# Half-array matmuls gathered in two groups per slot, longer key and value rows, and a reordered entry in a fused attention and routed feed-forward kernel

## The chip, the cores and the metric

The kernel runs on one core of a Trainium2 chip. The metric is the device time of the whole kernel in microseconds (us). All data start and end in the chip's main memory.

## What is computed

```python
q_n = q / (norm(q) + 1e-06); k_n = k / (norm(k) + 1e-06)      # q, k, v: (8, 12, 448, 64), float32
scores = q_n @ k_n.T / tau                                    # tau 0.1
attn = softmax(scores); x = attn @ v                          # then x: (8, 448, 768)
for b in range(8):                                            # routed feed-forward
    s = x[b] @ w_gate
    top = the 128 tokens of largest s
    h = relu(x[b, top] @ w1)                                  # w1: 768 x 1024
    out[b] = x[b]; out[b, top] += sigmoid(s[top]) * (h @ w2)  # w2: 1024 x 768
```

## The kernel before

The 12 heads of a batch are taken in pairs, so there are 48 pairs, six to a batch. The main loop has 49 **slots**. Slot i does the scores and exponentials of pair i and the product with the values (PV) of pair i-1, prepares pairs further on, and carries a piece of the routed feed-forward (MoE) of an earlier batch. The order on every engine is the order in which the code is written; PE, DVE, ACT, POOL and the SP queue each work through their own list and wait on semaphores.

The 448 keys of a head are cut into three blocks of 128 and a tail of 64. Tails of the two heads sit in the lower and the upper 64 partitions of one block. A matmul on a tail, or on 64-row heads, uses half the array: it has a `tile_position`. In a slot PE runs

- `scores(i, c)`, c = 0 to 2 (L264): two half-array matmuls of 448 columns each, one per head; c = 3 (L269) is one full matmul on both tails. Each writes a `sc` tile; there are two of these buffers.
- `pv(i-1, u)` (L290, L293): for each head u and each of four row blocks, a half-array tail matmul, then three full ones, 65 columns each: 8 tails and 24 full ones in a slot.
- `transposes(i+1)` (L238, L233): four half-array (64 by 64) and six full ones into `qkT_ps`, copied by DVE (`qkT_copy`, L253) for the next slot's scores.
- `sum_pe` (L185): eight full matmuls that sum squares for the norms of a pair five slots on, into the free half of `sc(i, 3)`; DVE reduces them (`sum_dve`, L191).

ACT does `exps(i, c)` (L277, L280), `square` (L178) and, once per three pairs, two short norm instructions (L200, L201). DVE does `pv_evac` (L304, L305), which empties the PV result, and the routing arithmetic: `gate` (L327), `rank_count` (L366). POOL does `scale` (L217), `values` (L224) and `pick`. SP issues the loads: a group of three pairs in nine transfers, q, k and v in one large and two small ones each.

MoE pieces hang in a table, `at(slot, place, ...)`. Places "A" and "B" carry PE blocks: `rank_rep` (L354), `select`, `gather` (L425), `ffn1` (L439), `ffn2` (L452). In a slot "A" comes after `scores(i, 2)`, and "B" at the end, after `scores(i+1, 0)`, which is issued ahead. All MoE blocks share one PSUM bank (`m_ps`). Before the loop, an entry of five pairs loads and norms what the first slots need; after it the last batch's MoE runs alone.

## Time and profile before

| | |
|---|---|
| median of 2 runs | 522.43 us (522.36 to 522.5) |
| the profiled run | 518.5 us |
| its span, first to last instruction | 516.7 us |
| busy: PE, ACT, DVE, POOL | 449.1, 203.4, 181.0, 175.4 us |
| granted TensorE clock, mean | 0.779 |

Busy times are unions over the span; a busy PE is not PE at its peak, since matmuls overlap in it. The granted clock is a share of 2.4 GHz, and 0.50 means 1.2 GHz. The clock's first record in this trace comes after 100 us; stretches ahead of it are shown as 1.00.

### The profile page before, as it was taken

The page shows a single profiled execution, that of the slowest core. Times are in us where ns is not written, and L with a number is a line of the kernel's source. Part 1 is how long each engine was busy: PE and PEld are TensorE (multiplying, and loading weights), DVE is VectorE, ACT ScalarE, POOL GpSimd, SP SyncE. Part 2 cuts the span into 40 slices and gives each one's busy share as a digit, 9 for nine tenths or more (in the row PEclk, how much of TensorE's full clock was granted, in tenths as well). Part 3 has the DMA queues.
Part 4 walks back from the last instruction along what each step waited for, and adds up shares of the span by engine and source line. Part 5 has one row for each costly group of instructions (what it writes and reads, how often), then busy time and mean ns, then how long its engine had stood idle before and what let it go on. Part 6 is the DMA issues. An engine that isn't in the chain of part 4 may idle for free.

```text
span 516.7 us, 8595 instructions
## 1 busy us (share of the span) xinstructions
PE 449.1 (87%) x3537; PEld 273.1 (53%) x3537; DVE 181.0 (35%) x471; ACT 203.4 (39%) x291; POOL 175.4 (34%) x268
## 2 busy tenths in 40 slices
PE   2599998989999799979999799979998999899372
PEld 1355554545656457545665466545664565446250
DVE  1122223342262424442443425342444225334420
ACT  2463535344445335453453434543354433223000
POOL 2460415332425323360633323451534243310501
PEclk9999999985698657985787659875698567669556
DMA  6999759250666039250837048431502060020702
GB/s 164 283 283 251 166 124 242 60 148 1 157 164 178 15 107 213 58 138 1 214 108 190 1 127 195 117 75 41 122 1 31 1 159 3 0 32 1 190 1 30
DMA packets 64487, 56.78 MB, mean 110 GB/s; under 512 B 21568, under 2 KB 59968, under 8 KB 63424
## 3 DMA queue, kind: packets, MB, share of 16 engines
q1 hardware_dynamic: 59248, 44.21, 29.8%
q0 software_dynamic: 4768, 11.80, 14.9%
q8 instruction: 27, 0.44, 0.3%
q10 hardware_dynamic: 432, 0.23, 0.1%
q14 instruction: 12, 0.10, 0.1%
HBM read 39.71 MB, written 14.16 MB: 104 GB/s over the span
## 4 chain that ended last, share of the span: by engine, by line
PE 79%; DVE 12%; ACT 3%; SPq 2%; DMA 2%; issue 1%; POOLq 0%; POOL 0%; DVEq 0%; ACTq 0%
PE o_ps L293 18%; PE o_ps L290 10%; PE sc L264 9%; PE qkT_ps L233 9%; PE qkT_ps L238 6%; PE m_ps L425 6%; PE m_ps L452 6%; PE m_ps L439 5%; PE sc L185 4%; DVE junk L366 4%; DVE junk L327 3%; PE sc L269 3%; ACT expS L280 2%; PE m_ps L354 2%; DVE qkT L253 2%; DMA qk_raw<-in_k_dram 2%
## 5 line engine op out<-in xcount | busy, mean ns | idle before, releaser
L277 ACT ACTIVATE expS<-sc 128x896 bf16<-128x896 f32 x144 | 128.5, 915 | 173.2 <-PE sc L264 173.1
L293 PE MATMUL o_ps<-vo,expS 128*128 128x65 bf16 (+1 forms) x1152 | 118.8, 220 | 0.0
L217 POOL TENSOR_TENSOR qkn<-qk_raw,rs 128x512 bf16<-128x512 f32 x96 | 88.8, 954 | 54.3 <-ACT expS L277 27.8
L264 PE MATMUL sc<-qkT 64*128 64x448 bf16 x288 | 69.4, 472 | 27.3 <-ACT expS L280 22.7
L290 PE MATMUL o_ps<-vo,expS 64*128 64x65 bf16 (+1 forms) x384 | 84.9, 221 | 0.0
L293 PEld LDWEIGHTS <-expS 128*128 128x128 bf16 (+1 forms) x1152 | 66.3, 112 | 31.8 <-issue 14.4
L304 DVE RECIPROCAL rden<-o_ps 128x8 f32<-128x8 f32 x48 | 10.0, 208 | 159.3 <-PE o_ps L293 159.3
L233 PE MATMUL qkT_ps<-iden_b,qkn 128*128 128x128 bf16 x288 | 58.7, 267 | 0.5 <-POOL qkn L217 0.5
L280 ACT ACTIVATE expS<-sc 128x448 bf16<-128x448 f32 x48 | 26.1, 543 | 73.0 <-DVE ss L191 69.9
L290 PEld LDWEIGHTS <-expS 64*128 64x128 bf16 (+1 forms) x384 | 39.0, 102 | 24.0 <-issue 0.3
L185 PE MATMUL sc<-sq,iden_b 128*128 128x112 bf16 x384 | 39.9, 274 | 11.1 <-ACT sq L178 11.1
L178 ACT ACTIVATE sq<-qk_raw 128x896 bf16<-128x896 f32 x48 | 45.5, 952 | 9.1 <-DMA qk_raw<-in_k_dram 9.1
L238 PE MATMUL qkT_ps<-iden_b,qkn 64*64 64x64 bf16 x192 | 45.7, 238 | 2.5 <-POOL qkn L217 2.5
L185 PEld LDWEIGHTS <-iden_b 128*128 128x128 bf16 x384 | 34.9, 132 | 20.5 <-issue 19.1
L253 DVE COPY qkT<-qkT_ps 128x960 bf16<-128x960 bf16 x48 | 31.6, 658 | 37.7 <-PE qkT_ps L233 37.7
L264 PEld LDWEIGHTS <-qkT 64*128 64x128 bf16 x288 | 16.8, 98 | 52.0 <-issue 46.2
L458 POOL DMA_INDIRECT out_dram<-oe,idx x8 | 13.5, 1689 | 77.4 <-DVE oe L412 41.9
L452 PE MATMUL m_ps<-w_sb,hT 128*128 128x384 bf16 x128 | 35.1, 438 | 5.0 <-DVE junk L366 2.3
L318 POOL DMA_DIRECT2D xh<-x_b x8 | 5.0, 620 | 101.1 <-DVE x_b L305 101.1
L439 PE MATMUL m_ps<-xeT,w_sb 128*128 128x128 bf16 x384 | 32.8, 261 | 1.3 <-DVE hT L408 0.8
L305 DVE TENSOR_TENSOR x_b<-o_ps,rden 128x512 f32<-128x512 f32 x48 | 33.2, 691 | 1.7
L439 PEld LDWEIGHTS <-w_sb 128*128 128x128 bf16 x384 | 29.8, 121 | 6.2 <-issue 6.1
(70 smaller groups left out, 375.3 us busy)
## 6 DMA issues: line engine op xcount, KB each, us to landing
out_dram<-x_b SPq DMA_DIRECT2D x8, 1152.0 KB, 4.3
qk_raw<-in_q_dram SPq DMA_DIRECT2D x15, 576.0 KB, 6.4
qk_raw<-in_k_dram SPq DMA_DIRECT2D x15, 576.0 KB, 6.7
v_raw<-in_v_dram SPq DMA_DIRECT2D x15, 576.0 KB, 6.2
xh<-x_b POOLq DMA_DIRECT2D x8, 576.0 KB, 10.9
w_sb<-in_moe_w_dram POOLq DMA_DIRECT2D x2, 1536.0 KB, 12.8
out_dram<-x_b SPq DMA_DIRECT2D x8, 192.0 KB, 8.6
qk_raw<-in_q_dram SPq DMA_DIRECT2D x30, 48.0 KB, 5.8
```

The lines of the kernel that those rows point to most:

```text
L178: nc.scalar.activation(sq_tiles[p], raw[gi % NRAW][0][:, :, g].rearrange("p a b d -> p a (b d)") [:, :, :NB7 * Dh], AF.Square)
L185: nc.tensor.matmul(out=dst[:, :2 * NB7 * D8], lhsT=iden_b, rhs=sq[:, :, s * D8:(s + 1) * D8], start=(s == 0), stop=(s == Dh // D8 - 1))
L217: nc.gpsimd.tensor_mul(kn[:, :, :nb, o:o + Dh], qk[:, :, g, b0:b0 + nb], rs[:, g, :, b0:b0 + nb].rearrange("p a (b o) -> p a b o", o=1) .t ...
L233: nc.tensor.transpose(out=qkT_ps[:, o:o + P], in_=kn[:, a, c], identity=iden_b)
L238: nc.tensor.transpose(out=qkT_ps[r, o:o + T], in_=kn[r, a, NC, :Dh], identity=iden_b[r, r], tile_position=(u * T, u * T))
L253: nc.vector.tensor_copy(qkT_tiles[p], qkT_ps[:, :W])
L264: nc.tensor.matmul(out=sc[:, u, :S], lhsT=qkT[r, KO + c * P:KO + (c + 1) * P], rhs=qkT[r, :S], start=True, stop=True, tile_position=(u * D ...
L277: nc.scalar.activation(ex[:, 2 * c:2 * c + 2], sc[:, :, :S], AF.Exp, scale=inv_tau)
L290: nc.tensor.matmul(out=o, lhsT=ex[r, TAIL, cols], rhs=vo[r, NC], start=True, stop=False, tile_position=(u * T, 0))
L293: nc.tensor.matmul(out=o, lhsT=ex[:, 2 * c + u, cols], rhs=vo[:, u * NS + c], start=False, stop=(c == NC - 1))
L439: nc.tensor.matmul(out=ps[:, f * CAP:(f + 1) * CAP], lhsT=w1_sb[:, t, fc * P:(fc + 1) * P], rhs=xeT[:, t], start=(t == 0), stop=(t == KD - 1))
L452: nc.tensor.matmul(out=ps[:, :ND], lhsT=hT[:, t], rhs=w2_sb[:, t, n * ND:(n + 1) * ND], start=(t == 0), stop=(t == KF - 1))
```

## The change

**PE.** In a slot, `scores(i, 0)` and `scores(i, 1)` now stand together, then all eight PV tails (`pv_tails`, two heads in turn), then the 24 full PV matmuls. `scores(i, 2)` and the four 64 by 64 transposes stand together, then `scores(i, 3)`, the six full transposes, the sums, and "B". `scores(i+1, 0)` is no longer issued ahead of "B". The tail matmuls of a head open the whole accumulation bank once (`start` for j = 0 only).

**Other engines.** `exps(i, 3)` is issued before the sums and their reduction. Place "D" is split: "D1" ahead of `pv_evac`, "D2" behind it and ahead of `qkT_copy`; gates and rank counts are spread over both. "A" now comes right after `pv_evac`. `pick` moves one slot earlier. Some evacuations of the last two batches go to ACT.

**Loads.** Keys and values take another assignment of tokens to partitions: four tokens (1024 B) or three (768 B) in a row, in four transfers of 64 partitions per load. Queries are as before. The entry norms three pairs instead of five, starts slot 0 at once, and PE runs 80 matmuls on zeros (`warm`).

```diff
+    NORMS = [(0, 1), (1, 2), (3, 2)]
+    while sum(NORMS[-1]) < N:
+        NORMS.append((sum(NORMS[-1]), min(3, N - sum(NORMS[-1]))))
+    nplace = {g0 + g: (n, g) for n, (g0, gn) in enumerate(NORMS) for g in range(gn)}
...
-        eng.dma_start(
-            out=dst.rearrange("p g (u c) d -> p (g u) (c d)", c=4)[:, :, :NC * Dh],
-            in_=src[b, h0:h0 + nh, 0:SM, :].rearrange("h (m c) d -> m h (c d)", c=NC))
+        if which == 0:
+            eng.dma_start(
+                out=dst.rearrange("p g (u c) d -> p (g u) (c d)", c=4)[:, :, :NC * Dh],
+                in_=src[b, h0:h0 + nh, 0:SM, :].rearrange("h (m c) d -> m h (c d)", c=NC))
+            for u in range(2):
+                eng.dma_start(
+                    out=dst[u * T:u * T + T, :, NC],
+                    in_=src[b, h0:h0 + nh, SM:S, :].rearrange(
+                        "(g h) p d -> p g h d", h=2)[:, :, u])
+            return
+
+
         for u in range(2):
-            eng.dma_start(
-                out=dst[u * T:u * T + T, :, NC],
-                in_=src[b, h0:h0 + nh, SM:S, :].rearrange(
-                    "(g h) p d -> p g h d", h=2)[:, :, u])
-
-
...
+            for half in range(2):
+                n = NS if half == u else NC
+                b0 = 0 if u == 0 else NB7 - n
+                t0 = 0 if half == u else NS * T
+                eng.dma_start(
+                    out=dst[half * T:half * T + T, :, b0:b0 + n]
+                    .rearrange("p g c d -> p g (c d)"),
+                    in_=src[b, h0:h0 + nh, t0:t0 + n * T, :].rearrange(
+                        "(g h) (p c) d -> p g h (c d)", h=2, c=n)[:, :, u])
...
+    load(0, 0, nc.sync)
+    load(0, 1, nc.scalar)
+    nc.scalar.preload_act_table_set("natural_log_exp_and_others")
+    load(1, 0, nc.sync)
+    load(1, 1, nc.sync)
+    load(0, 2, nc.sync)
...
-        for b0, nb, o in ((0, NS, 0), (NS, NC, Dh)):
-            nc.gpsimd.tensor_mul(
+        for eng, b0, nb, o in zip(engines or (nc.gpsimd, nc.gpsimd),
+                                  (0, NS), (NS, NC), (0, Dh)):
+            eng.tensor_mul(
                 kn[:, :, :nb, o:o + Dh], qk[:, :, g, b0:b0 + nb],
...
-        tail(0, 0)
-        full(0, 0)
-        tail(0, 1)
-        full(0, 1)
-        tail(1, 0)
-        full(0, 2)
-        tail(1, 1)
-        for c in range(NC):
-            full(1, c)
+        if part == 0:
+            for a in range(2):
+                for u in range(2):
+                    tail(a, u)
+        else:
+            for a in range(2):
+                for c in range(NC):
+                    full(a, c)
...
-    def pv(i, u):
+
+
+    def pv_tails(i):
         ex = exp_tiles[i]
         vo = vo_bufs[i % NB]
-        r = slice(u * T, u * T + T)
         for j in range(NS):
             n = rows(j)
-            cols = slice(j * P, j * P + n)
-            o = o_ps[:n, u, j * E:(j + 1) * E]
-            nc.tensor.matmul(out=o, lhsT=ex[r, TAIL, cols], rhs=vo[r, NC],
-                             start=True, stop=False, tile_position=(u * T, 0))
-            for c in range(NC):
-                nc.tensor.matmul(out=o, lhsT=ex[:, 2 * c + u, cols],
-                                 rhs=vo[:, u * NS + c], start=False, stop=(c == NC - 1))
+            for u in range(2):
+                r = slice(u * T, u * T + T)
+                nc.tensor.matmul(out=o_ps[:n, u, j * E:(j + 1) * E],
+                                 lhsT=ex[r, TAIL, j * P:j * P + n], rhs=vo[r, NC],
+                                 start=(j == 0), stop=False, tile_position=(u * T, 0),
+                                 skip_group_check=True)
+
+    def pv(i):
+        ex = exp_tiles[i]
+        vo = vo_bufs[i % NB]
+        for u in range(2):
+            for j in range(NS):
+                n = rows(j)
+                for c in range(NC):
+                    nc.tensor.matmul(out=o_ps[:n, u, j * E:(j + 1) * E],
+                                     lhsT=ex[:, 2 * c + u, j * P:j * P + n],
+                                     rhs=vo[:, u * NS + c], start=False,
+                                     stop=(c == NC - 1), skip_group_check=True)
...
+    for b in range(B - 2):
         s = HP * (b + 1)
...
+        for j, (d, w) in enumerate(((1, "D1"), (1, "D2"), (2, "D1"), (2, "D2"))):
+            at(s + d, w, gate, b, j)
+        at(s + 3, "P", rank_prep, b)
+        at(s + 3, "B", rank_rep, b)
+        for j in range(NS):
+            at(s + 4, "D1" if j < 2 else "D2", rank_count, b, j)
+        at(s + 4, "P2", pick, b)
+        at(s + 5, "A", select, b)
+        at(s + 5, "C", select_b, b)
+        at(s + 5, "B", gather, b, 0)
+        at(s + 6, "A", gather, b, 1)
+        at(s + 6, "B", ffn1, b, 0)
+        late = b < B - 3
+        at(s + 7, "B" if late else "A", ffn1, b, 1)
+        at(s + 7 + late, "B", ffn2, b, 0)
+        at(s + 8 + late, "A", ffn2, b, 1)
...
+    at(s + 2, "B0", rank_rep, b)
...
+    at(s + 6, "A", ffn1, b, 1, "A")
+    at(s + 6, "A", ffn2, b, 0, "A")
+    at(s + 6, "A", ffn2, b, 1, "A")
...
+    SQ = {}
+    for p in range(3, N):
+        SQ.setdefault({3: 0, 4: 0, 5: 1, 6: 1}.get(p, p - 5), []).append(p)
+    SW = 2 * NB7 * D8
...
+    warm(30)
...
+            warm(50)
+            scale(0, (nc.gpsimd, nc.vector))
...
+            scores(i, 0)
             scores(i, 1)
+        if prev:
+            pv_tails(i - 1)
+            pv(i - 1)
+        if live:
             exps(i, 0)
             exps(i, 1)
+            for p in SQ.get(i, []):
+                square(p)
+        run(i, "D1")
         if prev:
-            pv(i - 1, 0)
-            pv(i - 1, 1)
             pv_evac(i - 1)
-        if nxt:
-            transposes(i + 1)
-            qkT_copy(i + 1)
-        run(i, "D")
+        run(i, "A")
+        run(i, "D2")
+        run(i, "P2")
         if i + 2 < N:
             scale(i + 2)
             values(i + 2)
         if live:
             scores(i, 2)
-            if i + LA < N:
-                square(i + LA)
-            exps(i, 2)
-        run(i, "A")
+        if nxt:
+            transposes(i + 1, 0)
         if live:
             scores(i, 3)
-            if i + LA < N:
-                sc = sc_tiles[i, 3]
-                sum_pe(i + LA, sc[:, 1])
-                sum_dve(i + LA, sc[:, 1])
+        if nxt:
+            transposes(i + 1, 1)
+            qkT_copy(i + 1)
+        if live:
+            exps(i, 2)
+            sc = sc_tiles[i, 3]
             exps(i, 3)
-            gi, g = place.get(i + LA, (0, -1))
-            if g == GROUPS[gi][1] - 1:
-                norm_a(gi)
-                norm_b(gi)
+            for m, p in enumerate(SQ.get(i, [])):
+                dst = sc[:, 1, m * SW:(m + 1) * SW]
+                sum_pe(p, dst)
+                sum_dve(p, dst)
+                n, g = nplace[p]
+                if g == NORMS[n][1] - 1:
+                    norm_a(n)
+                    norm_b(n)
         run(i, "C")
-        run(i, "E")
-        if nxt:
-            scores(i + 1, 0)
+        run(i, "B0")
         run(i, "B")
```

On PE, at the end of the first slot with `rank_rep` (L354, now L384), before. L264 is `scores`, L290 a PV tail, L293 a full PV matmul.

```order
L264 LDWEIGHTS qkT [waits DVE_49]
L264 MATMUL sc<-qkT 128x448 [waits Activation_49]
...
L354 MATMUL m_ps<-diag,ones_f 128x448 [waits Pool_49]
L357 MATMUL m_ps<-gate_145,iden_f 128x4
...
L264 MATMUL sc<-qkT 128x448 [waits Activation_49]
...
L290 MATMUL o_ps<-vo_138,expS 128x65
L293 LDWEIGHTS expS
L293 MATMUL o_ps<-vo_138,expS 128x65
...
L290 MATMUL o_ps<-vo_138,expS 128x65
```

One score pair is issued ahead of the MoE block, one behind it, and tails alternate with runs of three. And now (L203 sums, L282 `scores`, L309 a tail, L321 a full PV matmul):

```order
L203 MATMUL sc<-sq,iden_b 128x112
L384 MATMUL m_ps<-diag,ones_f 128x448 [waits Pool_49]
L387 MATMUL m_ps<-gate_151,iden_f 128x4
L282 LDWEIGHTS qkT [waits DVE_49]
L282 MATMUL sc<-qkT 128x448 [waits PE_49]
...
L282 MATMUL sc<-qkT 128x448 [waits DVE_49]
...
L309 MATMUL o_ps<-vo_144,expS 128x65
...
L321 MATMUL o_ps<-vo_144,expS 128x65
```

All four score matmuls stand behind the MoE block, the tails follow them, and the full matmuls come in one run.

On PE, from the end of PV to the third and fourth scores in a plain slot, before (L238 and L233 are half and full transposes):

```order
L238 LDWEIGHTS qkn_136 [waits Pool_49]
L238 MATMUL qkT_ps<-iden_b,qkn_136 64x64
L233 LDWEIGHTS qkn_136 [waits Pool_49]
L233 MATMUL qkT_ps<-iden_b,qkn_136 128x128
...
L238 MATMUL qkT_ps<-iden_b,qkn_136 64x64
...
L233 MATMUL qkT_ps<-iden_b,qkn_136 128x128
...
L264 MATMUL sc<-qkT 128x448 [waits Activation_49]
...
L269 MATMUL sc<-qkT 128x448 [waits Activation_49]
```

Half and full transposes alternate there, ahead of the scores. The same stretch now, up to the sums (L257 and L252 are the transposes):

```order
L282 MATMUL sc<-qkT 128x448 [waits Activation_49]
...
L257 LDWEIGHTS qkn_142 [waits Pool_49]
L257 MATMUL qkT_ps<-iden_b,qkn_142 64x64
...
L287 MATMUL sc<-qkT 128x448 [waits Activation_49]
L252 LDWEIGHTS qkn_142 [waits Pool_49]
L252 MATMUL qkT_ps<-iden_b,qkn_142 128x128
...
L203 MATMUL sc<-sq,iden_b 128x112 [waits Activation_49]
```

The half transposes moved behind the third score pair, and the full ones follow the full score matmul without a half-array one between.

On DVE, the second slot with gates of a batch, before (L304, L305 `pv_evac`; L253 `qkT_copy`; L327 `gate`; L191 `sum_dve`):

```order
L304 RECIPROCAL rden<-o_ps 128x8 [waits PE_49]
L305 TENSOR_TENSOR x_b<-o_ps,rden 128x4x128 [waits DVE_49]
L253 COPY qkT<-qkT_ps 128x960 [waits PE_49]
L327 ISA junk,gate_145<-x_b,wg_b 128x768
L327 ISA gate_145 128x1
L327 ISA junk,gate_145<-x_b,wg_b 64x768 [waits DVE_49]
L327 ISA gate_145 64x1
L191 TENSOR_REDUCE ss<-sc 128x14 [waits PE_49]
```

Both gates stand behind the copy there. The same slot now (L334, L335; L271; L357; L209, in the same roles):

```order
L357 ISA junk,gate_151<-x_b,wg_b 128x768 [waits DVE_49]
L357 ISA gate_151 128x1
L334 RECIPROCAL rden<-o_ps 128x8 [waits PE_49]
L335 TENSOR_TENSOR x_b<-o_ps,rden 128x4x128 [waits DVE_49]
L357 ISA junk,gate_151<-x_b,wg_b 64x768
L357 ISA gate_151 64x1
L271 COPY qkT<-qkT_ps 128x960 [waits PE_49]
L209 TENSOR_REDUCE ss<-sc 128x14 [waits PE_49,Activation_49]
```

One gate moved ahead of `pv_evac` and one ahead of `qkT_copy`, and the reduction of the sums now waits on ACT.

## Rows read from the trace of the kernel before

**Rows 1.** The page, part 4: the chain that ended last, by engine.

```profile
PE 79%; DVE 12%; ACT 3%; SPq 2%; DMA 2%; issue 1%; POOLq 0%; POOL 0%; DVEq 0%; ACTq 0%
```

**Rows 2.** Stretches, a slot each: length; PE PEld DVE ACT POOL busy; clock; DMA; GB/s.

```profile
40.29:48.88 8.59, 8.13 (x58) 4.57 (x58) 1.83 (x4) 3.91 (x5) 0.56 (x1) 1.00 1.12 229
...
150.03:157.70 7.67, 7.05 (x66) 4.42 (x65) 3.57 (x8) 4.39 (x6) 3.44 (x8) 1.00 0.05 13
...
167.22:176.92 9.70, 6.77 (x58) 4.11 (x57) 4.41 (x12) 3.92 (x5) 5.24 (x9) 0.78 0.19 35
176.92:188.09 11.17, 11.17 (x82) 6.45 (x82) 3.11 (x10) 4.15 (x6) 0.00 (x0) 0.50 0.00 0
```

**Rows 3.** Timeline of PE, an early slot: start, length, instruction, [idle before].

```profile
48.77 0.26 PE L238 MATMUL qkT_ps<-iden_b,qkn 64*64 64x64 bf16 x1
...
50.62 0.56 PE L264 MATMUL sc<-qkT 64*128 64x448 bf16 x2
...
51.46 0.95 PE L185 MATMUL sc<-sq,iden_b 128*128 128x112 bf16 x8
...
53.68 0.26 PE L290 MATMUL o_ps<-vo,expS 64*128 64x65 bf16 x1
53.87 0.35 PE L293 MATMUL o_ps<-vo,expS 128*128 128x65 bf16 x3
...
57.37 0.26 PE L238 MATMUL qkT_ps<-iden_b,qkn 64*64 64x64 bf16 x1
```

**Rows 4.** Timeline of PE, a later slot.

```profile
149.93 0.21 PE L238 MATMUL qkT_ps<-iden_b,qkn 64*64 64x64 bf16 x1
...
151.26 0.36 PE L264 MATMUL sc<-qkT 64*128 64x448 bf16 x2
...
151.76 0.56 PE L185 MATMUL sc<-sq,iden_b 128*128 128x112 bf16 x8
...
152.93 1.47 PE L452 MATMUL m_ps<-w_sb,hT 128*128 128x384 bf16 x8
...
154.90 0.19 PE L290 MATMUL o_ps<-vo,expS 64*128 64x65 bf16 x1
155.02 0.27 PE L293 MATMUL o_ps<-vo,expS 128*128 128x65 bf16 x3
...
157.60 0.21 PE L238 MATMUL qkT_ps<-iden_b,qkn 64*64 64x64 bf16 x1
```

**Rows 5.** The chain in order of time, MoE blocks on PE: start, length.

```profile
163.21 0.95 PE m_ps L354 x2
...
181.52 2.61 PE m_ps L425 x16
...
193.42 2.68 PE m_ps L439 x24
...
470.25 1.46 PE m_ps L439 x24
...
482.68 1.86 PE m_ps L354 x2
```

**Rows 6.** Waits: us in total, times, longest.

```profile
ACT expS L280 <- DVE ss L191: 69.9, 43, 3.2
```

**Rows 7.** Groups by line and shape, DVE: busy, mean ns | idle before.

```profile
L305 DVE TENSOR_TENSOR x_b<-o_ps,rden 128x512 f32<-128x512 f32 x48 | 33.2, 691 | 1.7
...
L253 DVE COPY qkT<-qkT_ps 128x960 bf16<-128x960 bf16 x48 | 31.6, 658 | 37.7 <-PE qkT_ps L233 37.7
...
L327 DVE CUSTOM_DVE_ANT_0 junk<-x_b,wg_b 128x768 bf16<-128x768 f32 x21 | 20.0, 952 | 0.3
```

**Rows 8.** The chain again, the square that ends the entry.

```profile
19.39 0.96 ACT sq L178
```

**Rows 9.** Line L304, the first evacuation instruction of each pair: first and last start.

```profile
L304 DVE RECIPROCAL rden<-o_ps x48: 206/208/209, 31.7 to 478.8; 128x8 f32<-128x8 f32 x48
```

**Rows 10.** Loads: KB each, median us from issue to landing.

```profile
qk_raw<-in_k_dram SPq DMA_DIRECT2D x15, 576.0 KB, 6.7
```

More of the change, by code (lines that the diff above doesn't have):

```diff
@@ L184, in sum_pe @@
         for s in range(Dh // D8):
-            nc.tensor.matmul(out=dst[:, :2 * NB7 * D8], lhsT=iden_b,
+            nc.tensor.matmul(out=dst, lhsT=iden_b,
                              rhs=sq[:, :, s * D8:(s + 1) * D8],
@@ L226, with transposes @@
     qkT_tiles = {}
-    def transposes(p):
+    def transposes(p, part):
         kn = kn_bufs[p % NB]
@@ L414, in evac, with gather @@
             nc.scalar.activation(dst, src, func, scale=scale)
-    def gather(b, part):
+    def gather(b, part, eng="D"):
         sel, xh = st[b]["sel"], xh_tiles[b]
@@ new lines @@
+        late = b < B - 3
+        at(s + 7, "B" if late else "A", ffn1, b, 1)
+        at(s + 7 + late, "B", ffn2, b, 0)
+        at(s + 8 + late, "A", ffn2, b, 1)
+    b, bb = B - 2, B - 1
+    s = HP * bb
+    for j, (d, w) in enumerate(((0, "D2"), (1, "D1"), (1, "D1"), (1, "D2"))):
+        at(s + d, w, gate, b, j)
+    at(s + 2, "P", rank_prep, b)
+    at(s + 2, "B0", rank_rep, b)
+    for j in range(NS):
+        at(s + 3, "D1" if j < 2 else "D2", rank_count, b, j)
+    at(s + 3, "P2", pick, b)
```

153 lines of the change are left out of this document (60 added, 93 removed).

## The prediction

> **What bounds the kernel now.** I first read the page's chain of waits: 79% of the span is PE [rows 1], so PE's own work and PE's order set the time. Then I cut the span into slots, from one first evacuation instruction (L304) to the next. There are 48, the first at 31.7 us and the last at 478.8 [rows 9], so the span of 516.7 is 31.7 of entry, 47 intervals of 9.51 on average, and 37.9 behind the last one. The intervals differ by two things, the MoE blocks in them and TensorE's clock [rows 2]: a plain slot takes 8.59 with PE busy for 8.13, a slot with one feed-forward block 7.67, a slot with two gathers 11.17.
>
> The clock has to be read from lengths early on. The stretch at 40.29 is shown with a granted clock of 1.00 [rows 2], but the eight sums take 0.95 in the slot after it, and 0.56 a hundred us later, where 1.00 is shown too [rows 2 to 4]. A feed-forward block of 24 matmuls takes 2.68 at 193.42, soon after a slot at 0.50, against 1.46 late in the kernel [rows 2, 5], much the same ratio. So the early part ran at the lower level, 1.2 GHz, and the early slots are slow for that. Later the kernel changes between the levels: the slot at 176.92 has PE busy for its whole length and a clock of 0.50, the one at 150.03 has 1.00 [rows 2].
>
> Last come PE's rows inside a slot. PV takes 2.70 at the high level (154.90 to 157.60) and 3.69 at the low one (53.68 to 57.37), though it is only 32 matmuls of 65 columns [rows 3, 4]. Three full ones in a row need 0.27 (0.35 low) from first start to last end, while one alone takes about 0.19 to 0.24: they start about 0.04 (0.06) apart. The step from a tail to a full matmul takes 0.12 (0.19). PE pays for changes between half and full array, sixteen of them in PV and eight in the transposes.
>
> **The change part by part.**
>
> *PV.* After: 24 full ones and 8 tails at 0.04 and one change of 0.12, 0.96 + 0.32 + 0.12 + 0.05 for the narrow blocks = 1.45; it saves 1.25 at the high level. At the low one 24 x 0.06 + 8 x 0.06 + 0.19 = 2.1, saving 1.6. No row shows tails of the two heads next to each other. The two score matmuls of a pair end in 0.36 together, so half matmuls of different halves do overlap [rows 4]; the bounds are 0.16 for the eight (in pairs) and 8 x 0.12. I take 0.32.
>
> The Trainium skill speaks against this term (TensorE: Matmul & The Clock Gate, "Back-to-back issue gap": in a stream of weight load and matmul pairs, about 81 ns each for 128 columns). By that figure the 24 would take 1.9 us, an estimate, and the total would come out a few us later. This trace does not agree: 24 feed-forward matmuls of 128 columns in 1.46 us are 61 ns each [rows 5].
>
> *Transposes.* 1.33 now at the high level, 1.85 at the low one (149.93 to 151.26, 48.77 to 50.62) [rows 3, 4]. After: six full ones at 0.061 (0.112), four half ones at 0.04 (0.05), one change: 0.65 (1.07). It saves 0.68 (0.78).
>
> *PE in a plain slot.* High: 7.05 busy at 150.03, less the feed-forward block of 1.47 [rows 2, 4], is 5.6; less 1.93 is 3.65. Low: 8.13 less 2.4 is 5.75.
>
> *The new chain.* Now ACT matters. The order makes `exps(i, 3)` come before the sums, and both use the tile `sc(i, 3)`. Before, with the opposite order, `exps(i, 3)` waited for the reduction of the sums, 69.9 us in 43 slots [rows 6]; that wait goes. What is late next is its mirror image: the sums wait for `exps(i, 3)`, and the "B" block, the next score pairs and their exponentials are queued behind the sums on PE. One round is: first score pair 0.36 (0.56), ACT's five instructions 3.91 in a plain slot [rows 2], sums 0.56 (0.95), four hand-overs of about 0.05. That is 5.0 (5.6). PE alone needs 3.65 (5.75), so a plain slot takes 5.0 at the high level, bound by ACT and the hand-overs, and 5.7 at the low one, bound by PE. Before, `scores(i+1, 0)` was ahead of "B" and ACT worked under "B"; now "B" adds its length in full. B blocks of a batch, high: `rank_rep` 0.95, a gather of 16 (estimated from the 24 in 1.46) 1.0, three feed-forward blocks at 1.46, together 6.3 or 1.06 a slot; low: 1.86 + 2.61 + 3 x 2.68 = 12.5, 2.1 a slot [rows 5]. "A" blocks lie beside ACT's exponentials; I charge 0.2 (0.4). Two norm instructions every third slot add about 0.15, and DVE and POOL in the slots of rank counts and `pick` 0.15: DVE's row from PV's end to the next scores is evacuation 0.69 + 0.21, a gate 0.95, the copy 0.66 [rows 7], 2.5, and fits in 5.0 behind a PV that ends at about 2.1. Sum: **6.55 us a slot with MoE at the high level, 8.45 at the low one.** Bounds: no extra waits at all 6.0; nothing below, since ACT's 3.91, the sums and "B" are rows.
>
> *Which level.* Runs of full matmuls become the rule, which speaks for the high level: the blocks that ran at 1.46 to 1.47 did so behind such runs. Against it: in a high slot PE ends its transposes after about 3.0 us and waits until 4.5 for the sums, and in the slot at 167.22, where PE was busy for 6.77 of 9.70, the clock was 0.78 and then 0.50 [rows 2]. I take a mixture of two thirds high: 7.2 a slot with MoE, 5.4 a plain one.
>
> *Entry.* Before, the squares of pair 3 start at 19.39, when their keys arrive [rows 8]. The bytes ahead of them are the same after; slot 0 now runs before, and these squares come inside it. From 19.39: two squares 1.8, two exponentials 1.4, two sums 1.9, scores and PV 3.1: the first evacuation at 27.7. Slot 1 then waits for group 3, which is asked for no earlier, and the second comes at 35.4, where before it was at 31.7 + 8.6 = 40.3. Longer rows carry the same bytes in eleven transfers a group instead of nine; 576 KB land in 6.7 us [rows 10] against three slots of lead, so I count nothing, hidden by that lead. The 80 warm matmuls cost nothing either while PE waits for the first keys; without that cover the 50 would cost 50 x 0.11 = 5.6. Splitting `scale(0)` over POOL and DVE and moving one exponential of the gates are below 1 us.
>
> *End.* 37.9 before. In the last slot three feed-forward blocks now share the single bank with the last `rank_rep`, and their evacuations go through ACT: some 4 us more. Evacuations in turn on ACT and DVE give back about 1. I take 41.
>
> *Sum.* 35.4 to the second evacuation, 7 plain intervals at 5.4 = 37.8, 39 with MoE at 7.2 = 280.8, end 41: a span of 395. The span of before stands to the median of the runs as 516.7 to 522.43, a factor of 1.011: **about 399 us**.
>
> **The rivals.**
>
> *The clock stays high* (0.25): 35.4 + 7 x 5.0 + 39 x 6.55 + 40 = 365.9, or 370 us. For it: blocks and runs are denser than anything in the early slots. Against: the pause of about 1.5 in each slot. With no extra waits, 6.0 a slot, it is 349.
>
> *The clock stays low* (0.15): 35.4 + 7 x 5.7 + 39 x 8.45 + 43 = 447.9, or 453 us. For it: the early slots had PE busy for 8.13 of 8.59 and never left that level.
>
> *The gathering does not do what it says* (0.08): each full PV matmul waits for its weight load. The wait is then bounded by a feed-forward matmul of 0.112 at the low level, so 24 x 0.07 = 1.7 more, of which ACT's slack of about 1.1 in the middle of the slot hides most; 0.6 a slot comes through, 28 us: 427. Three starts in 0.27 speak against it [rows 4].
>
> *Slower than before* (0.03): the loads. Each transfer on SP's queue waits for the one eight before it, so a group of eleven takes 11/8 of a landing time. It decides from a landing of 15.7 us, when that equals three slots of 7.2; for more than 533 us the slots must be 10.6, a landing of 23. Rows show 6.7 [rows 10], so 64-partition transfers would have to be over three times slower.
>
> **How the numbers follow.** The forecast has 0.47, its own range 378 to 425. The rest (0.02) is spread out. From 358 to 450 lie the forecast, most of the high case, the ungathered case and half of the low one, about 0.8. A change of 2% is about what a measurement of this kernel can tell from none. All cases but the last are faster by more, so 0.95; slower 0.03; the rest 0.02.
>
> **What would show it.** In the profile after: PV in a slot at 1.4 to 1.5 us (high), the transposes at about 0.65, the wait of the fourth exponential for the reduction gone, and in its place a wait of the sums' matmuls for `exps(i, 3)`; plain slots between 5.0 and 5.7; the mean clock between 0.6 and 0.9. Wrong would be: sums that start without waiting, a clock at one level throughout, or slots bounded by DVE, POOL or the loads.

## The result and the profile after

The changed kernel takes **370.57 us**, median of 2 runs (369.96 to 371.18), against 522.43: a ratio of 0.709 with a 95% interval of 0.704 to 0.714. The forecast was 399 and its range 358 to 450. The time is that of the rival in which the clock stays high (370). The medians here and below leave out runs that lie more than 1.5% above the fastest of the same kernel; ranges have every run.

| stage of the span | forecast | profile after |
|---|---|---|
| first, second evacuation of PV, at | 27.7, 35.4 | 30.8, 38.5 |
| 7 plain intervals | 37.8 | 40.2 |
| 39 intervals with MoE | 280.8 (7.2 each) | 249.6 (6.40 each) |
| behind the last evacuation | 41 | 41.1 |
| span | 395 | 369.4 |

The first evacuation instruction of each pair again (line L334 now, L304 in [rows 9]): 48, from 30.8 to 328.3. Below they are counted from 0: evacuation 0 ends the entry, and evacuation 8 the plain intervals.

```profile
L334 DVE RECIPROCAL rden<-o_ps x48: 196/207/209, 30.8 to 328.3; 128x8 f32<-128x8 f32 x48
```

Part 4 of the page, the chain that ended last; it answers to [rows 1]. PE had 79%, and no engine now has half.

```profile
PE 34%; ACT 19%; DVE 14%; DMA 13%; issue 12%; SPq 3%; POOL 2%; POOLq 1%; DVEq 0%; ACTq 0%
```

Stretches of the changed kernel, with the columns of [rows 2]: first the stages (entry, first interval, 7 plain ones, 38 with MoE, end; the 39th with MoE, 6.35, lies between the last two), then five neighbouring slots.

```profile
0.00:30.82 30.82, 17.92 (x186) 14.88 (x186) 6.08 (x28) 12.32 (x19) 10.64 (x24) 0.82 0.78 195
30.82:38.47 7.65, 6.78 (x67) 4.64 (x65) 2.11 (x6) 4.77 (x7) 5.29 (x9) 0.50 1.07 259
38.47:78.71 40.24, 31.07 (x401) 20.90 (x399) 18.54 (x42) 27.40 (x41) 19.65 (x29) 0.81 1.07 246
78.71:321.96 243.25, 200.65 (x2764) 141.27 (x2763) 168.81 (x363) 148.99 (x217) 134.26 (x193) 0.96 0.64 148
328.31:369.40 41.09, 18.25 (x140) 12.20 (x139) 7.66 (x27) 3.62 (x7) 8.98 (x14) 0.73 0.31 70
...
161.68:166.74 5.06, 3.80 (x60) 2.61 (x58) 3.03 (x9) 3.89 (x7) 4.33 (x7) 1.00 1.04 235
166.74:172.93 6.19, 5.55 (x83) 4.04 (x82) 4.60 (x13) 4.29 (x10) 2.49 (x4) 1.00 0.64 165
172.93:182.51 9.58, 7.78 (x122) 5.99 (x122) 7.37 (x9) 6.09 (x9) 8.35 (x11) 1.00 0.84 214
182.51:186.96 4.45, 2.89 (x54) 2.25 (x51) 3.98 (x11) 1.56 (x2) 0.48 (x1) 1.00 1.06 279
186.96:195.16 8.20, 7.69 (x66) 4.48 (x65) 3.94 (x10) 4.63 (x9) 1.96 (x6) 0.58 0.42 106
```

A slot without a block takes 5.06, and PE is busy in 3.80 of it. The granted clock over the 38 MoE slots is 0.96: if 1.00 is the high level and 0.50 the low one, 8% of the stretch was low. The five rows also show something that the prediction had not foreseen: once in a batch an interval of 9.58 stands beside one of 4.45. Here a low stretch comes right behind that pair. It does so behind two of the five pairs (0.78 and 0.58); behind the other three the clock is 1.00, and 7.78 us of the low time lie in one slot near the end (314.18 to 321.96).

PE's timeline of one slot; it answers to [rows 4].

```profile
177.22 0.55 PE L282 MATMUL sc<-qkT 64*128 64x448 bf16 x4
177.61 0.40 PE L309 MATMUL o_ps<-vo,expS 64*128 64x65 bf16 x8
177.94 1.27 PE L321 MATMUL o_ps<-vo,expS 128*128 128x65 bf16 x24
179.14 0.36 PE L282 MATMUL sc<-qkT 64*128 64x448 bf16 x2
179.44 0.25 PE L257 MATMUL qkT_ps<-iden_b,qkn 64*64 64x64 bf16 x4
179.62 0.36 PE L287 MATMUL sc<-qkT 128*128 128x448 bf16 x1
179.82 0.50 PE L252 MATMUL qkT_ps<-iden_b,qkn 128*128 128x128 bf16 x6
181.47 0.55 PE L203 MATMUL sc<-sq,iden_b 128*128 128x112 bf16 x8 [1.16 <-ACT expS L298]
```

PV, from 177.61 to 179.14, is 1.53 (2.70 before); the transposes are 0.25 + 0.50 (1.33 before). The sums now wait for the fourth exponential. The list of waits has that as a whole; the wait of [rows 6] is not in it.

```profile
ACT expS L295 <- PE sc L282: 92.0, 55, 4.6
...
PE sc L203 <- ACT expS L298: 41.4, 41, 5.9
```

The pair of 9.58 and 4.45 is told by two engines' timelines between 175 and 183. VectorE:

```profile
177.32 0.69 DVE L438 TENSOR_SCALAR hT<-m_ps 128x512 bf16<-128x512 f32 x1 [1.00 <-PE m_ps L469]
177.93 4.64 DVE L357 CUSTOM_DVE_ANT_0 junk<-x_b,wg_b 128x768 bf16<-128x768 f32 x1
182.51 0.20 DVE L334 RECIPROCAL rden<-o_ps 128x8 f32<-128x8 f32 x1
```

GpSimd:

```profile
174.16 0.63 POOL L348 DMA_DIRECT2D xh<-x_b  x1 [4.93 <-DVE x_b L335]
...
175.33 1.86 POOL L236 TENSOR_TENSOR qkn<-qk_raw,rs 128x512 bf16<-128x512 f32 x2
177.11 0.57 POOL L243 CAST vo<-v_raw 128x448 bf16<-128x448 f32 x1
177.63 1.84 POOL L236 TENSOR_TENSOR qkn<-qk_raw,rs 128x512 bf16<-128x512 f32 x2
179.42 0.55 POOL L243 CAST vo<-v_raw 128x448 bf16<-128x448 f32 x1
179.93 1.82 POOL L236 TENSOR_TENSOR qkn<-qk_raw,rs 128x512 bf16<-128x512 f32 x2
181.71 1.27 POOL L243 CAST vo<-v_raw 128x448 bf16<-128x448 f32 x1
```

GpSimd first idles for 4.93 ahead of a store of x that waits for the evacuation, then has three pairs' scale and values in a row. The first gate of the batch (0.95 in [rows 7]) takes 4.64, nearly as long as that row lasts, and the evacuation of a PV that ended at 179.14 stands behind it until 182.51. It happens in five batches (4641 to 4675 ns). In the first batch the profile has the gate wait 4.49 for its weights `wg_b` beside the same row, and the interval is 9.52.

### The profile page after: what moved, and what is told of

The parts are those of the page before. It is cut to its first block, busy times and chain, and to the rows that moved or that the text cites. A ratio compares the mean times of both kernels' runs of the same rounds, so it can differ in the third digit from the quotient of the medians.

```text
span 369.4 us, 8858 instructions
## 1 busy us (share of the span) xinstructions
PE 281.0 (76%) x3617; PEld 198.5 (54%) x3617; DVE 206.6 (56%) x476; ACT 198.5 (54%) x291; POOL 178.8 (48%) x267
## 4 chain that ended last, share of the span: by engine, by line
PE 34%; ACT 19%; DVE 14%; DMA 13%; issue 12%; SPq 3%; POOL 2%; POOLq 1%; DVEq 0%; ACTq 0%
ACT expS L295 12%; DMA qk_raw<-in_q_dram 7%; PE o_ps L321 7%; PE m_ps L482 6%; PE m_ps L455 5%; PE sc L282 5%; PE sc L203 4%; DVE junk L357 4%; ACT sq L196 3%; DMA wg_b<-in_moe_w_gate_dram 3%; DVE junk L396 3%; SPq L114 3%; ACT expS L298 3%; PE m_ps L469 3%; DVE qkT L271 2%
## 5 line engine op out<-in xcount | busy, mean ns | idle before, releaser
L236 POOL TENSOR_TENSOR qkn<-qk_raw,rs 128x384 bf16<-128x384 f32 (+1 forms) x95 | 91.8, 1032 | 26.0 <-DVE rs L226 12.8
L321 PE MATMUL o_ps<-vo,expS 128*128 128x65 bf16 (+1 forms) x1152 | 64.5, 202 | 0.0
L203 PE MATMUL sc<-sq,iden_b 128*128 128x112 bf16 x384 | 29.5, 226 | 45.8 <-ACT expS L298 41.4
L282 PE MATMUL sc<-qkT 64*128 64x448 bf16 x288 | 50.5, 383 | 15.2 <-DVE qkT L271 13.2
L321 PEld LDWEIGHTS <-expS 128*128 128x128 bf16 (+1 forms) x1152 | 51.2, 104 | 10.0
L203 PEld LDWEIGHTS <-iden_b 128*128 128x128 bf16 x384 | 25.7, 105 | 51.8 <-issue 51.1
L357 DVE CUSTOM_DVE_ANT_0 junk<-x_b,wg_b 128x768 bf16<-128x768 f32 (+3 forms) x32 | 48.3, 1510 | 4.6 <-DMA wg_b<-in_moe_w_gate_dram 4.5
L271 DVE COPY qkT<-qkT_ps 128x960 bf16<-128x960 bf16 x48 | 31.3, 652 | 14.8 <-PE qkT_ps L252 14.8
L334 DVE RECIPROCAL rden<-o_ps 128x8 f32<-128x8 f32 x48 | 9.9, 206 | 45.7 <-PE o_ps L321 45.6
L243 POOL CAST vo<-v_raw 128x448 bf16<-128x448 f32 x48 | 35.1, 731 | 0.5 <-DMA v_raw<-in_v_dram 0.5
L335 DVE TENSOR_TENSOR x_b<-o_ps,rden 128x512 f32<-128x512 f32 x48 | 33.2, 691 | 1.7
L209 DVE TENSOR_REDUCE ss<-sc 128x14 f32<-128x112 f32 x48 | 13.0, 272 | 31.8 <-PE sc L203 31.3
L366 POOL TENSOR_TENSOR diag<-iden_f,gate 128x512 f32<-128x512 f32 x8 | 8.9, 1117 | 41.4 <-DVE gate L357 41.4
L282 PEld LDWEIGHTS <-qkT 64*128 64x128 bf16 x288 | 12.6, 95 | 29.7 <-DVE qkT L271 16.6
L405 POOL TENSOR_SCALAR sel<-iota_r,rank 128x128 bf16<-128x128 bf16 (+1 forms) x32 | 22.7, 854 | 10.8 <-DVE junk L396 10.1
```

The lines of the kernel that those rows point to most:

```text
L203: nc.tensor.matmul(out=dst, lhsT=iden_b, rhs=sq[:, :, s * D8:(s + 1) * D8], start=(s == 0), stop=(s == Dh // D8 - 1))
L236: eng.tensor_mul(kn[:, :, :nb, o:o + Dh], qk[:, :, g, b0:b0 + nb], rs[:, m, :, b0:b0 + nb].rearrange("p a (b o) -> p a b o", o=1) .to_broa ...
L243: nc.gpsimd.tensor_copy(vo_bufs[p % NB][:, :, :Dh], raw[gi % NRAW][1][:, g, :NB7])
L271: nc.vector.tensor_copy(qkT_tiles[p], qkT_ps[:, :W])
L282: nc.tensor.matmul(out=sc[:, u, :S], lhsT=qkT[r, KO + c * P:KO + (c + 1) * P], rhs=qkT[r, :S], start=True, stop=True, tile_position=(u * D ...
L321: nc.tensor.matmul(out=o_ps[:n, u, j * E:(j + 1) * E], lhsT=ex[:, 2 * c + u, j * P:j * P + n], rhs=vo[:, u * NS + c], start=False, stop=(c ...
```

## The experiments

**The theories.** A: the gathering is the gain, through shorter PE work and through the high level. B: the gain is the new order (exponentials ahead of the sums, blocks ahead of the next scores, entry), and the gathering lies in ScalarE's shadow. For the 9.58: GpSimd's row keeps the gate out, or the gate only shows another wait. "38 slots" below is the stretch between evacuations 8 and 46, with its mean granted clock, in the run that has the trace (436.7 us for PV alone, 380.7 for the transposes alone). The kernel before took 505.3 to 523.9 beside these runs, with medians of 517.5 to 519.8, so a few us between two rows of the table are not resolved. The edits are shown shortened.

| kernel | us, median (lowest to highest) | 38 slots, us | clock there |
|---|---|---|---|
| before | 522.4 | 368.1 | 0.74 |
| all but the gathering | 464.5 (461.6 to 464.5) | 317.0 | 0.77 |
| PV alone as it was | 430.3 (430.1 to 442.9) | 294.5 | 0.82 |
| gathering alone | 394.0 (393.9 to 398.5) | 282.8 | 0.77 |
| sums first | 385.0 (383.6 to 386.0) | 254.6 | 0.81 |
| transposes alone as they were | 378.3 (376.0 to 383.1) | 245.6 | 0.95 |
| changed | 370.6 (370.0 to 371.2) | 243.3 | 0.96 |
| old entry | 370.0 (369.2 to 371.5) | 242.1 | 0.97 |
| short rows | 367.2 (365.0 to 368.9) | 242.1 | 0.97 |
| gate behind the evacuation | 364.6 (362.9 to 365.9) | 237.9 | 0.98 |
| gate behind the copy | 360.7 (357.3 to 361.4) | 237.3 | 0.95 |
| entry, stores and gate | 355.3 (355.0 to 360.9) | 229.0 | 0.98 |
| stores of x behind values | 352.8 (351.9 to 360.9) | 228.2 | 1.00 |
| entry, stores and gate, scores ahead | 381.1 (379.8 to 383.4) | 256.9 | 0.89 |

**PV as it was, the rest changed.**

```diff
-            pv_tails(i - 1)
-            pv(i - 1)
+            # per (u, j): the half matmul (start=True), then its three full ones
```

> The changed kernel, with only PV as it was: each (u, j) opens its own sum with its half-array matmul and adds its three full ones, where pv stands now; everything else as changed. Theory A (the gathering is the gain, and the short slots keep the clock high): PV takes 2.7 us in place of about 1.5 in each slot; 39 MoE slots of 6.40 become 7.65 and the plain ones rise by about 0.6, so 424 at the same clock, and 440 to 480 if the granted clock falls from 0.89 to 0.8 or less. Rival B (the gain is the new order of exps, sums and scores, and the entry; the gathered PV only lies in the shadow of ScalarE): PV still reads 2.7, but the time is 375 to 390 and the clock stays near 0.89.

430.3 us, ratio to before 0.834 (0.819 to 0.849). PE's timeline has the old alternation at the old price: PV from 243.70 to 246.40, 2.70.

```profile
243.70 0.19 PE L314 MATMUL o_ps<-vo,expS 64*128 64x65 bf16 x1
243.82 0.27 PE L317 MATMUL o_ps<-vo,expS 128*128 128x65 bf16 x3
...
246.40 0.33 PE L411 MATMUL m_ps<-tokc,sel 128*128 128x2 bf16 x4
```

The stretch of that slot, and the whole 38 slots:

```profile
240.43:246.51 6.08, 4.82 (x60) 3.23 (x58) 2.94 (x9) 3.91 (x5) 4.33 (x6) 1.00 1.01 270
...
91.56:386.06 294.50, 274.85 (x2764) 185.03 (x2763) 157.21 (x364) 150.85 (x216) 131.45 (x190) 0.82 0.50 115
```

Theory A holds and B falls, though the time lies between A's two cases (424, and 440 to 480). A plain slot at the high level is 6.08 against 5.06; 1.02 over 47 intervals would be 48 of the 60 us lost. The remaining 12 stand beside a lower clock: 0.80 over the whole of the two runs that make the median, against 0.89.

**The transposes as they were, the rest changed.**

```diff
-        if part == 0: the four half transposes
-        else: the six full ones
+        if part == 0: return
+        tail, full, tail, full, tail, full, tail, full, full, full
```

> The changed kernel, with only the transposes in their old alternation of half and full, all behind scores(i, 3). Theory A: 0.68 us more on TensorE in each slot (1.33 against 0.65), in 39 MoE slots that are bounded by TensorE: 371 + 27 = 397, half that (384) if the transposes' wait for the scale hides part. Rival B: they lie before the wait for exps, so they are hidden: 370 to 374. The granted clock stays at 0.85 or more in both.

378.3 us, below A's bounds and above B's. The 38 slots hardly move (245.6 against 243.3), as B expected. In the traced run the loss is ahead of them: evacuation 8 comes at 87.6 in place of 78.7, and the early slots stay at the low level with PE busy throughout, 6.75 each for four of them:

```profile
38.86:65.84 26.98, 26.96 (x230) 16.59 (x228) 8.57 (x20) 16.16 (x24) 8.07 (x11) 0.50 1.05 222
```

That is the rival in which the clock stays low, for 50 us. Why it stays low there is not shown.

**Both as they were.** The two edits above together.

> The changed kernel with PV and the transposes both in their old alternation; the order of the slot, the entry and the loads stay as changed. Theory A: 1.25 + 0.68 us more per slot over 39 MoE slots and less over the plain ones: 450 at the same clock, and up to 500 if the clock falls to about 0.7 as the longer slots idle; most of the 152 us gained is lost again. Rival B: 380 to 395, so that four fifths of the gain stay.

464.5 us, ratio 0.898 (0.887 to 0.910): all the rest of the change is worth 55 us without the gathering. On top of PV, the transposes cost 34 and not 8: PE is busy in 312.5 of the 317.0 us of the 38 slots, so nothing hides them.

**The gathering alone, in the kernel before.**

```diff
-            pv(i - 1, 0)
-            pv(i - 1, 1)
+            pv_tails(i - 1)
+            pv(i - 1)
```

(and `transposes` with its four half ones ahead of its six full ones)

> The kernel before with the gathering alone: PV's eight half-array matmuls opened together and the transposes in two groups, at the places where pv and transposes stood; the order of the slot, the entry, the loads and the MoE's places stay as before. Theory A (the gathering is worth the same anywhere): 464 - 371 = 94 us, the difference between the changed kernel with and without it, so 428. Interaction (it pays in full only if ScalarE no longer waits for the sums behind scores(i, 3)): the slots stay bounded by that wait, and TensorE idles and falls to its low level: 470 to 500. A third: the gathering alone brings the high level and nearly all of the gain, 385 or less.

394.0 us, ratio 0.768 (0.765 to 0.771): 125 us, more than either of the first two cases expected and less than the third. The parts do not add up: 125 and 55 alone, 152 together. The wait of [rows 6] is still there, with 36 of its 43 times:

```profile
ACT expS L277 <- DVE ss L191: 66.5, 36, 4.5
```

So that wait did not hold the kernel before; PE did. Plain slots take 4.35 here, less than the changed kernel's 4.75 to 5.06. From here to the changed kernel it is another 23 us; the next run shows what the order of sums and exponentials has in that. The new places of the MoE pieces and the evacuations on ACT were not undone alone.

**Sums ahead of the fourth exponential again.**

```diff
-            exps(i, 3)
             for m, p in enumerate(SQ.get(i, [])):
                 sum_pe, sum_dve
+            exps(i, 3)
```

> The changed kernel with the sums put ahead of exps(i, 3) again, as before; the instructions are the same, only who waits for whom in the tile of scores(i, 3) is turned round. If the wait that the prediction let go was part of the bound: sums (0.4 us) and VectorE's reduction (about 0.6) and its hand-overs go back between scores(i, 3) and exps(i, 3), 1.2 to 1.5 us for 45 slots, of which those bounded by TensorE hide some: 400 to 435, with rows of expS waiting for ss near 60 us. Rival: TensorE has the sums done while ScalarE still runs exps 0 to 2, so that nothing waits: 366 to 374, and TensorE's 41 us of waits for expS at the sums are gone, with no gain since they lay in ScalarE's shadow.

385.0 us, ratio 0.750 (0.743 to 0.756), between the two. The wait is back in full:

```profile
ACT expS L298 <- DVE ss L209: 75.8, 43, 12.5
```

76 us of waiting cost 14 us. Plain slots get shorter by it, 4.42 (46.44 to 50.86) against 4.75. The loss is in the MoE slots: 11 us over 38, at a clock of 0.81. Some 6 more go to one interval of 15.73 in which a gate waits 12.9 for `wg_b`, long after GpSimd's row has ended, and 3 come back in the early slots. So the order of sums and exponentials is worth some 8 us without that one wait, and those lie in the MoE slots, beside a lower clock.

**The first gate moved behind the evacuation.**

```diff
-        enumerate(((1, "D1"), (1, "D2"), (2, "D1"), (2, "D2")))
+        enumerate(((1, "D2"), (1, "D2"), (2, "D1"), (2, "D2")))
```

> The changed kernel with the first gate of each batch (b below 6) moved from in front of pv_evac to behind it in the same slot, beside the second gate; nothing else. Port theory (the 4.64 us of that gate, against 0.95 of every other, are VectorE kept from SBUF by GpSimd's row of scale and values): the gate then falls behind GpSimd's row or beside its last operations, and the six intervals of 9.5 fall to about 6: 3 x 6 = 18 to 21 us less, 350 to 353. Rival (the long interval is a wait that only shows at the gate: the stores of x, the DMA issue that GpSimd holds, or the next transposes waiting for the late scale): evacuations in these slots stay at 9.5, time 368 to 372.

364.6 us, ratio 0.707 (0.697 to 0.716). The interval did fall to 6.32, but the next grew:

```profile
94.14:100.46 6.32, 5.68 (x91) 4.33 (x90) 2.88 (x6) 3.91 (x7) 5.09 (x7) 1.00 1.03 315
100.46:107.68 7.22, 4.99 (x83) 3.91 (x81) 6.72 (x11) 3.75 (x6) 3.74 (x5) 1.00 1.06 211
```

6.32 + 7.22 against 9.58 + 4.45: the port theory had the place and not the size (6 us for 18 to 21), since the slot behind the long one had been short by what the long one did ahead of time. The gate still takes 2.47 to 2.50 there and the second 1.19, beside the end of GpSimd's row. The two ratios overlap, so the 6 us rest on the traces: six slots at the high level take 37.5 in place of 37.95.

**The first gate behind `qkT_copy`.**

```diff
-        for j, (d, w) in enumerate(((1, "D1"), (1, "D2"), (2, "D1"), (2, "D2"))):
+        for j, (d, w) in enumerate(((1, "D3"), (2, "D1"), (2, "D1"), (2, "D2"))):
...
             qkT_copy(i + 1)
+        run(i, "D3")
```

> The changed kernel with the first gate of each batch behind qkT_copy of its slot, and the second at the front of the next, so that GpSimd's row has ended when the gate runs. Port theory: no gate is above 1.3 us, the interval of 9.58 falls to 6 to 6.5 and the next one stays under 6.5, which is 1.5 us per batch better than with the gate behind pv_evac (6.32 + 7.22): 352 to 360. Rival: the pair of slots costs 13.5 whatever the gate does, as GpSimd's late scale holds the transposes: 363 to 367.

360.7 us, ratio 0.701 (0.691 to 0.711). The pair is 6.32 + 6.64 = 12.96, better than 13.5, and the slot behind it takes 5.55 in place of 6.10; but the gate still takes 1.5 to 1.7 us (1.98 in the first batch) and not under 1.3, and the time is just above the port theory's range. One slot ran at the low level, 8.75 long where its like in other batches takes 6.2:

```profile
198.01:206.76 8.75, 8.68 (x83) 5.93 (x83) 4.54 (x13) 4.96 (x9) 2.13 (x3) 0.50 0.46 108
```

**GpSimd's stores of x behind scale and values.**

```diff
         xh = xp.tile([P, NS, D], BF16, name="xh")
-        nc.gpsimd.dma_start(... x_b ...)   # twice, in "D2", ahead of scale and values
+    # store_xh(b): the same two, run behind values(i + 2)
```

> The changed kernel with GpSimd's two casting stores of x (xh) issued behind scale and values of their slot in place of ahead of them; the gates stay where they are. If the row of six GpSimd operations that meets the gate comes from GpSimd being held up by those two issues (they wait for pv_evac), the row breaks up: the first gate of a batch falls from 4.64 to under 2 us and the interval from 9.58 to about 6.3, of which the next slot gives back most, as the pair 9.58 + 4.45 became 6.32 + 7.22 with the gate moved: 3 to 12 us less, 358 to 367. If the row comes from elsewhere (the late scale of the slot before), the gate stays at 4.6 and the time at 369 to 372.

352.8 us, the best of these single edits and below both expectations. The gate still takes 2.4 to 2.9 and not under 2, and the intervals are 7.3 to 7.8 and 4.6 to 5.1, 12.4 together:

```profile
93.34:100.64 7.30, 6.66 (x102) 4.95 (x101) 5.09 (x9) 4.90 (x8) 6.99 (x10) 1.00 0.93 263
100.64:105.74 5.10, 3.94 (x72) 3.27 (x69) 4.08 (x11) 2.76 (x4) 0.48 (x1) 1.00 1.03 204
...
76.13:304.33 228.20, 192.91 (x2764) 137.69 (x2763) 156.56 (x363) 149.43 (x218) 133.00 (x193) 1.00 0.68 159
```

So a third of GpSimd's row came from the two issues that wait for `pv_evac`: two pairs stand in a row now and not three. In this run the 38 slots run at 1.00 throughout and take 6.0 each, as much as the prediction's bound without extra waits. Six slots of a batch take 36.3 here and 36.3 with the gate behind the copy, against 37.95 in the changed kernel: freeing the gate is worth 1.6 us a batch, some 8 in all, by either edit. The rest of the 18 stands beside the clock of 1.00 and one late interval (9.69 in the changed kernel, 7.42 here).

**The old entry.**

```diff
-    warm(30); norms of pairs 0 to 2; warm(50); pairs 3 to 6 squared in slots 0 and 1
+    for p in range(5): square, sum_pe, sum_dve, norm   # ahead of the loop
```

> The changed kernel with the entry of before: five pairs are squared, summed and normed ahead of the loop, no warm matmuls, group 0's values loaded ahead of group 1, and pairs from 5 on are squared five slots ahead; the slot itself stays as changed. Theory (the reordered entry costs time: it puts the squares, sums and norms of pairs 3 to 6 into slots 0 and 1, and lets TensorE start the slots at its low level): in the run with the gathering alone, which has this entry, evacuations 1 and 5 stand at 33.6 and 51.0 against 38.5 and 58.0 of the changed kernel, so 7 us less: 362 to 365. Rival, the prediction's own (the shorter entry brings the first evacuation forward by 4 us, and nothing is lost behind it): 371 to 376.

370.0 us, ratio 0.718 (0.710 to 0.725): no difference, so the theory is out; the rival's 371 is just missed. Evacuation 0 stands at 32.7 here and at 30.8 in the changed kernel, evacuation 1 at 37.9 and 38.5: what the new entry wins ahead of slot 0 is lost in it. My 7 us came from the run with the gathering alone, where evacuations 1 and 5 stand at 33.6 and 51.0; here they stand at 37.9 and 58.9 with the same entry. What I had put down to the entry lies in the early slots.

**Keys and values in short rows.**

```diff
-        if which == 0:
+        if True:
```

> The changed kernel with keys and values loaded in the rows of before (four blocks of 64 numbers as the queries are, and the rest in single rows), nothing else. The prediction counted the longer rows at nothing, since a load of 576 KB lands within a fraction of the three slots that it has: 368 to 373. Rival: with slots of 6 us in place of 9.5 the queue has less room, and 21568 packets below 512 B in place of 9824 bring scale and squares late or wg_b later: 375 to 390, with waits for qk_raw or v_raw in the steady part.

367.2 us, ratio 0.712 (0.704 to 0.720), the same within the intervals, and just below the expected range. The trace shows more than the ratio: the squares of pairs 3 and 4, which wait for their keys, start 3 us earlier than in the changed kernel (first row), and evacuation 0 stands at 27.9 in place of 30.8.

```profile
22.34 1.79 ACT L196 ACTIVATE sq<-qk_raw 128x896 bf16<-128x896 f32 x2 [4.35 <-DMA v_raw<-in_v_dram]
...
19.45 1.79 ACT L196 ACTIVATE sq<-qk_raw 128x896 bf16<-128x896 f32 x2 [3.08 <-DMA qk_raw<-in_k_dram]
```

The seven other traces with long rows and this entry have these squares at 21.0 to 22.4. So the longer rows bring nothing and cost 2 to 3 us in the entry, as far as one trace without them shows. This run also tells what `wg_b` was worth. The first gate of the first batch, in the changed kernel and here:

```profile
66.10 1.51 DVE L357 CUSTOM_DVE_ANT_0 junk<-x_b,wg_b 128x768 bf16<-128x768 f32 x1 [4.49 <-DMA wg_b<-in_moe_w_gate_dram]
...
58.14 6.30 DVE L357 CUSTOM_DVE_ANT_0 junk<-x_b,wg_b 128x768 bf16<-128x768 f32 x1
```

Here nothing waits for `wg_b`, the gate takes 6.30 beside GpSimd's row instead, and the interval is 9.53 as against 9.52. In the changed kernel the wait for `wg_b` therefore cost nothing; the row did.

**Three edits together.** The old entry, the stores behind values, the first gate behind `qkT_copy`.

> The changed kernel with three edits together: the entry of before, the casting stores of x behind scale and values, and the first gate of a batch behind qkT_copy. If the three add up: 7 of the entry, 14 of the stores (the run with them alone was 356.7) and 1 to 2 of the gate: 343 to 350. If the entry's part is not there or the pieces overlap: 351 to 357.

355.3 us, ratio 0.689 (0.681 to 0.698): faster than the changed kernel, whose interval begins at 0.704, but not than the stores alone; the pieces overlap, as the second expectation had it. No gate is slow any more:

```profile
L359 DVE CUSTOM_DVE_ANT_0 junk<-x_b,wg_b 128x768 bf16<-128x768 f32 x21 | 20.0, 951 | 0.2
```

That the mean is 951 ns here and 1857 in the changed kernel, and that this brings nothing beyond the stores alone (mean 1391), says that a gate of 2.4 to 2.9 no longer costs anything: six slots of a batch take 36.3 here too.

**Next scores ahead of the blocks.**

```diff
         run(i, "C")
+        if nxt: scores(i + 1, 0)
         run(i, "B0")
```

(and not at the start of the next slot)

> The kernel of the last run (old entry, stores of x behind values, first gate behind qkT_copy) with one more edit: scores(i+1, 0) are issued ahead of the blocks B0 and B at the end of a slot, as before, in place of behind them at the start of the next slot. The prediction's step: in the changed order the next scores queue behind the sums and the blocks, and ScalarE idles from exps(i, 3) to exps(i+1, 0), 1.17 us (156.75 to 157.92) in a plain slot of that run, and longer where there is a block. If that idle time bounds the slot: plain slots go from 5.06 to the 4.4 that the run with the gathering alone had, MoE slots of 6.2 to 6.6 come down to TensorE's 5.5 to 5.9 busy time, 0.4 us over 47 slots: 333 to 342. Rival (the slot is TensorE's, and the early scores only put the blocks behind them, with one more change between half and full array): 353 to 358.

381.1 us: 26 **slower**, outside both expectations. Waits of PE, matmuls:

```profile
PE sc L282 <- DVE qkT L271: 13.4, 19, 1.8
```

and of its weight loads:

```profile
PEld L282 <- DVE qkT L271: 20.6, 29, 2.6
```

In the run without this edit they are 1.9 and 4.4. The matmuls' waits lie inside those of their weight loads, so PE's waiting grew by 16 us and not by the sum; the sums' wait for `exps(i, 3)` fell by 10 (35.8 to 25.9). PE's timeline of one slot shows how:

```profile
248.54 0.55 PE L203 MATMUL sc<-sq,iden_b 128*128 128x112 bf16 x8 [0.77 <-ACT expS L298]
249.53 0.36 PE L282 MATMUL sc<-qkT 64*128 64x448 bf16 x2 [0.44 <-DVE qkT L271]
249.82 1.80 PE L457 MATMUL m_ps<-sel,xh 128*128 128x128 bf16 x16
```

`scores(i+1, 0)` needs the copy `qkT`; put first, it makes PE wait for 0.44, and the gather of 1.80 that could have covered the wait is queued behind it. At the high level six slots take 37.8 in place of 36.3, about 11 us for the whole; the other 15 stand beside a granted clock of 0.89 in place of 0.98. ScalarE's idle 1.17 us, which I had taken for the bound, was not it.

## Why the prediction was right, and where it was off

- **PV.** Right: 1.45 expected, 1.53 measured; the saving at the high level is 1.17 (1.25 expected). The eight half matmuls start in 0.33 (177.61 to 177.94; 0.32 taken). The undone edit shows 1.02 of it in a plain slot.
- **The rival that gathering does not do what it says** is out: 60 us come back when PV alone is undone.
- **Transposes.** 0.75 for the 0.65 expected. At the high level they are hidden; they count where PE bounds the slot.
- **The turned wait.** Right in kind: the wait of [rows 6] goes, and the sums wait 41.4 us in its place. Turned back, the kernel loses 14 us, 6 of them in one wait for `wg_b`, though 76 us of waiting return.
- **The slot's length.** 5.0 for a plain one at the high level, 5.06 measured. 6.55 for one with MoE, 6.40 measured, in which the pairs of 9.58 and 4.45 and the 8% at the low level are included. Whole batches at 1.00 take 37.95, 6.33 a slot, and with the gate freed 36.3, 6.05. Two errors of the sum nearly cancel: a gather takes 1.79 at the high level and not 1.0, while the small charges (0.2, 0.15 and 0.15 a slot) do not show, since 6.05 is 1.0 above a plain slot and "B" alone was put at 1.06.
- **A wait that the sum did not have.** It took the gate at 0.95 and let DVE's row fit in 5.0. Once a batch the gate takes 4.64 beside GpSimd's row, and the slot is bounded by DVE, one of the prediction's own signs of being wrong. It is worth 1.6 us a batch.
- **The step that was furthest off is "Which level"**: the mixture of two thirds high. It was 92% high. 39 x (7.2 - 6.40) = 31 us, less 5.5 by which entry and plain slots were late, is the difference of the spans. At the sum's own prices (6.55 and 8.45) the level is 19 of the 31; the other 12 are slots shorter than priced. I read PE's pause ahead of the sums as a reason for the low level. It is there (1.16 and 0.64 us in the slots shown), and slots with 3.80 of 5.06 busy keep 1.00. The slot at 0.58 follows one with PE busy in only 2.89 of 4.45, but three others with 2.86 to 2.88 are followed by 1.00. Where the stores' edit eases the long pairs, the whole stretch shows 1.00; with the gate behind the copy, which eases them as much, one slot is at 0.50. What decides the level inside a slot stays **open**: before and the gathering alone have PE busy for 93% and 88% of the 38 slots at 0.74 and 0.77, the changed kernel for 82% at 0.96. Busy time is itself longer at the low level, but busy share alone does not tell the level ahead.
- **Entry.** 3 us late, all of it ahead of the first evacuation (30.8 for 27.7); the interval behind it took 7.65, as the sum had it (35.4 - 27.7). The squares of pairs 3 and 4 start at 22.34 and not at 19.39. With short rows they start at 19.45, and the first evacuation stands at 27.9: the sum was right but for the longer rows. Undoing the entry changes nothing, so in this kernel the reordering's value was as good as zero, and not the 4.0 that the sum gave it (31.7 to 27.7).
- **Loads.** Counted at nothing, "hidden by that lead". In the slots that holds: undoing the rows leaves the 38 slots at 242.1 for 243.3. In the entry there is no such lead, and there the eleven transfers in place of nine go with the 3 us just named. One interval of 9.52 (58.02 to 67.54) among the plain ones has a gate that waits for `wg_b`, but the run with short rows has 9.53 without that wait.
- **End.** 41 expected, 41.1 measured.
- **Luck.** That the high case gives 370 is in part luck: its span is 365.9, against 369.4 with slots shorter and the other stages longer than in it, and the factor of 1.011 that makes 370 of it was 1.003 this time. Two of the sums are off by little: two thirds of 5.0 and a third of 5.7 are 5.2 and not 5.4, and the case without extra waits comes to 348 and not 349.
- **B in full.** The sum charged the blocks' whole length, and the old place of the scores looks cheaper by that. The last run shows that it is not: the blocks cover the copy.
